# One change to a gated mix of two attentions: the output projection's two halves placed together in every second slot

## The chip, the cores and the metric

The kernel runs on one core of a Trainium2 chip. The metric is the device time of one execution in microseconds (us). Beside plain runs there is one profiled execution, and every row of a trace below comes from it. Engines are named as the profile names them: PE multiplies matrices, PEld loads its weights, DVE, ACT and POOL work on vectors, and SP issues most of the DMAs.

## The reference, cut to what matters

Two attentions read the same `x` (2048 rows, 512 columns, 32 heads of 16) and are mixed row by row with a gate. A works in four blocks of 512 rows with a causal mask and adds a memory term; B is plain attention over all 2048 rows.

```python
g = _sigmoid((x * gate_w).sum(-1, keepdims=True))
a = _A_ref(x, A_wq, A_wk, A_wv, A_wo, A_beta)   # (softmax(q k^T/4 + mask) v, mixed with memory) @ wo
b = _B_ref(x, B_wqkv, B_wo)                     # softmax(q k^T/4) v  @ wo
return g * a + (1 - g) * b
```

The last step of each attention is a projection by a 512x512 matrix (`A_wo`, `B_wo`). The gate is applied to the rows ahead of it, so one row block of the output is the sum of two projections, one for A and one for B. These are the two "halves" of the title.

## The kernel before, in words

After a first part that makes queries, keys and values (up to 335 us in the trace), the work goes through 32 **slots**, `k` = 0 to 31. A slot handles one B unit and one A unit; a unit is four heads of one block of 512 query rows. Within a slot, 37 **groups** follow each other, all issued by the same loop over `n`, so that the order on every engine is the order of this program text:

- groups 0 to 31 are of the B unit, 32 to 36 of the A unit. Each begins with `t_group` (L516 to L538): two matmuls, one for each of two heads, write scores into two PSUM banks (L528), and ACT takes their exponentials into `raw` (L534). On A units POOL then masks (L537).
- Then come tasks from `plan`. In most groups that is one `s_b` (L467 to L476) for the next slot's B unit: a pair of score matmuls into a bank pair `sbk` (L474) and a maximum over them on DVE (L476, rows with `mxb`). In A groups it is `s_a` (L442 to L463).
- Then come the tasks of `ex[k][0]`, made by `extras` (L876). **The output projection is one of them.**
- Then `pv` (L540 to L551) multiplies exponentials with values into one bank, `pvb` (L550). In group 0 this ends the A unit of the slot before, and `fin_copy` (L553) copies the bank out on DVE (L557, `pvs`). In group 1 there is no `pv` in slots 1 to 30; from group 2 on there is one for the new B unit.

The scores and the projection share three PSUM banks, `T3` (two `tb` and one `mb`). `bank` and `misc` hand out the one used longest ago, so a new user waits until the last reader of that bank is done.

The projection has these parts:

- `out_split(c, t)` (L608): at the end of every even slot from 8 on, ACT copies 128 normalised rows for A and B to `oh` (L609, 128x1024) and POOL takes the remainder into `ol` (L610).
- `out_mm(c, t, a)` (L612): twelve matmuls into one bank (L616), `oh` with the weights' high part `wh`, then `oh` with `wl`, then `ol` with `wh`, four each. For `a` = 0 ACT copies the bank to `yo` (L620). For `a` = 1 DVE adds the bank to `yo` (L623) and SP stores 128 output rows (L624).

Before the change, slot `k` from 9 to 30 runs one half in group 1: `a` = 0 in odd slots, `a` = 1 in even ones. Slot 31 runs one half in group 1 and the other in group 28. The last four row blocks have a path of their own behind the slots (`tail_mm`).

Other steps that the prediction names: `fin_load`, `fin_rec`, `fin_bc` and `fin_norm` (L563 to L595) bring a finished unit's sums through DRAM and normalise them (DVE L574 to L578, POOL L590 and L595); `m_chain` (L480) makes the maxima of the next slot in four short DVE operations (L485 to L495).

Of the kernel before, what the change touches and what calls it, by code (L numbers as in the profile page):

```python
# [29 lines left out]
OMI = 14  # L30
# [4 lines left out]
def gated_mix_kernel(ctx, tc, xt, wq, wk, wv, wo, beta, wqkv, wob, gate_w, out):  # L35
# [622 lines left out]
    def todo(fn, *a):  # L658
        return lambda: fn(*a)
# [90 lines left out]
    for blk in range(16):  # L750
# [9 lines left out]
        n = blk + 1 + (c == 2)  # L760
# [114 lines left out]
    def extras(k):  # L875

        pre, post = {}, {}
        if not k:
            for n in range(4):
                pre[2 * n] = [fill[n - 4]]  # L880
        post[2 * S_LAST + 4] = [todo(m_rows, k + 1)]
        for n, at in [(k - 9, 1)] + [(23, 2 * OMI)] * (k == 31):
            if n >= 0:
                pre[at] = [todo(out_mm, n // 8, n // 2 % 4, n % 2)]
        return pre, post

    def beside(k, it):
# [26 lines left out]


    ex = [extras(k) for k in range(32)]
    plan = {}

# [103 lines left out]
```

## Time and profile before

| | us |
|---|---|
| median of 3 runs | 1959.34 |
| lowest, highest | 1958.81, 1960.34 |
| the profiled execution's own time | 1956.4 |
| its span, first to last instruction | 1954.7 |
| begin of slot 0, begin of slot 31 | 335.36, 1883.63 |

The span is cut into slots at the first score matmul of a B unit that follows one of an A unit. A row of a timeline gives the start in us from the span's start, the duration, the engine, the line of the kernel, the operation with what it writes and reads, the shape, the number of merged instructions, and in brackets how long the engine had been idle and whose end it waited for. A row of a table by stretches gives begin and end, the length, and then each engine's busy time with its instruction count.

### The profile page before, as it was taken

The numbers are of one execution on the slowest core, as the hardware profiler recorded it, in microseconds if no ns is written. First come the engines' busy times: TensorE is split into PE (matmuls) and PEld (weight loads), VectorE is DVE, ScalarE is ACT, GpSimd is POOL, SyncE is SP. The second block draws the span as 40 slices with busy tenths as digits, with TensorE's granted clock in tenths as the row PEclk, the third lists the DMA queues.
The fourth block names the chain that finished last, engine by engine and source line by source line (L and its number), as shares of the span: only waits on it lengthen the run. The fifth ranks groups of instructions, "written<-read, shape, count | busy, mean of one in ns | idle before, by whom it ended". The sixth has DMA issues, their size and how long they took to land.

```text
span 1954.7 us, 43539 instructions
## 1 busy us (share of the span) xinstructions
PE 1930.3 (99%) x17485; PEld 939.3 (48%) x17485; DVE 1629.9 (83%) x1798; ACT 1433.4 (73%) x2699; POOL 275.8 (14%) x497
## 2 busy tenths in 40 slices
PE   7999999999999999999999999999999999999999
PEld 5887777444344444444444444444444444444445
DVE  7135766899999999999999999999999999999942
ACT  4233333688888888888888888888888888888884
POOL 5201000012120101111111111111111111111022
PEclk9999999999999999999999999999999999999999
DMA  7666655644444444343435453444354444434111
GB/s 218 170 205 188 198 192 178 156 98 115 98 115 93 106 91 109 81 111 80 114 87 115 87 115 87 113 87 115 87 115 87 109 86 96 101 88 106 48 50 58
DMA packets 163790, 222.49 MB, mean 114 GB/s; under 512 B 39916, under 2 KB 90556, under 8 KB 157828
## 3 DMA queue, kind: packets, MB, share of 16 engines
q1 hardware_dynamic: 159284, 211.41, 43.7%
q0 software_dynamic: 3248, 8.03, 2.1%
q8 instruction: 138, 2.26, 0.5%
q14 instruction: 64, 0.52, 0.1%
q10 hardware_dynamic: 1056, 0.26, 0.1%
HBM read 147.95 MB, written 68.16 MB: 111 GB/s over the span
## 4 chain that ended last, share of the span: by engine, by line
PE 95%; DVE 3%; ACT 1%; SPq 1%; DMA 1%; issue 0%; DVEq 0%; ACTq 0%
PE pvb L550 33%; PE tb L528 17%; PE sbk L474 12%; PE mb L528 9%; PE tb L304 4%; PE sbk L452 3%; PE tb L616 2%; PE mb L304 2%; PE sbk L287 1%; DVE mxb L476 1%; PE tb L287 1%; PE pvb L304 1%; PE mb L616 1%; PE sbk L456 1%; PE mb L287 1%; PE pvb L287 1%
## 5 line engine op out<-in xcount | busy, mean ns | idle before, releaser
L476 DVE TENSOR_REDUCE mxb<-sbk 128x2 f32<-128x1024 f32 x1024 | 1222.3, 1222 | 67.3 <-PE sbk L474 63.1
L534 ACT ACTIVATE raw<-tb 128x512 f32<-128x512 f32 x1555 | 887.5, 598 | 152.9 <-PE tb L528 89.6
L550 PE MATMUL pvb<-raw,vb 128*17 128x256 f32 (+1 forms) x8072 | 639.3, 388 | 0.0
L534 ACT ACTIVATE raw<-mb 128x512 f32<-128x512 f32 x782 | 467.6, 598 | 79.5 <-PE tb L528 44.8
L528 PE MATMUL tb<-qb,xh 64*128 64x512 f32 x872 | 331.6, 495 | 1.7 <-ACT raw L534 1.7
L550 PEld LDWEIGHTS pvb<-raw,vb 128*17 128x17 f32 x8072 | 134.4, 95 | 340.1 <-issue 336.6
L474 PE MATMUL sbk<-xh,qb 64*128 64x512 f32 x1344 | 281.5, 395 | 2.7 <-DVE mxb L476 1.8
L528 PE MATMUL mb<-qb,xh 64*128 64x512 f32 x445 | 220.6, 496 | 0.0
L537 POOL TENSOR_SCALAR_AFFINE_SELECT raw<-raw 128x256 f32<-128x256 f32 (+1 forms) x320 | 115.5, 361 | 709.6 <-ACT raw L534 701.7
L528 PEld LDWEIGHTS tb<-qb,xh 64*128 64x128 f32 x872 | 124.7, 183 | 179.6 <-issue 89.9
L528 PE MATMUL tb<-qb,kb 64*128 64x512 f32 x470 | 179.5, 496 | 1.3 <-DVE st L314 0.8
L460 DVE TENSOR_REDUCE mx<-sbk 128x2 f32<-128x768 f32 (+1 forms) x128 | 136.7, 1090 | 22.9 <-PE sbk L456 18.3
L474 PE MATMUL sbk<-kb,qb 64*128 64x512 f32 x704 | 146.4, 398 | 0.0
L474 PEld LDWEIGHTS sbk<-xh,qb 64*128 64x128 f32 x1344 | 138.3, 186 | 7.4 <-DVE mxb L476 5.0
L528 PEld LDWEIGHTS mb<-qb,xh 64*128 64x128 f32 x445 | 81.3, 183 | 95.2 <-issue 50.4
L590 POOL TENSOR_TENSOR o<-o,d 128x512 f32<-128x512 f32 x31 | 39.7, 1281 | 545.6 <-DMA d<-rd 461.9
L528 PEld LDWEIGHTS tb<-qb,kb 64*128 64x128 f32 x470 | 68.2, 183 | 100.1 <-issue 52.6
L528 PE MATMUL mb<-qb,kb 64*128 64x512 f32 x234 | 116.1, 496 | 0.0
L550 PE MATMUL pvb<-raw,va 128*17 128x256 f32 (+2 forms) x1280 | 94.7, 384 | 0.8 <-ACT pvs L559 0.8
L452 PE MATMUL sbk<-ka,qa 64*128 64x256 f32 (+3 forms) x512 | 88.2, 358 | 1.1
L528 PE MATMUL tb<-qa,ka 64*128 64x512 f32 (+3 forms) x339 | 79.5, 372 | 0.0
L311 ACT ACTIVATE st<-tb 128x512 fp32r<-128x512 f32 x33 | 19.8, 599 | 80.2 <-DVE phi L310 40.5
(284 smaller groups left out, 1837.6 us busy)
## 6 DMA issues: line engine op xcount, KB each, us to landing
xh<-dB SPq DMA_DIRECT2D x38, 512.0 KB
vb<-vdB SPq DMA_DIRECT2D x16, 1088.0 KB
dB<-st SPq DMA_DIRECT2D x64, 256.0 KB
dA<-st SPq DMA_DIRECT2D x64, 256.0 KB
pd<-pvs SPq DMA_DIRECT2D x64, 256.0 KB
kb<-dB SPq DMA_DIRECT2D x22, 512.0 KB
xh<-dB SPq DMA_DIRECT2D x38, 256.0 KB
qb<-dB SPq DMA_DIRECT2D x64, 128.0 KB
```

Source lines behind the costliest of these rows:

```text
L287: nc.tensor.matmul(b, lhs, WV[wi][:, k, :], start=n == 0, stop=n == 11)
L304: nc.tensor.matmul(b, WS[ws][w][wi][:, k, :], (XH, XL)[xi][c][:, k, :], start=n == 0, stop=n == 11)
L452: nc.tensor.matmul(b[:, j, c0:c0 + n], q_of(u)[r, p, i * 128:(i + 1) * 128], k_of(u, p)[r, :n], start=True, stop=False)
L460: nc.vector.tensor_reduce(m[:, :, p, i], b[:, :, :n], axis=AX.X, op=OP.max)
L474: nc.tensor.matmul(b[:, j], q_of(u)[r, p, i * 128:(i + 1) * 128], k_of(u, p)[r, kc * C:(kc + 1) * C], start=True, stop=True)
L476: nc.vector.tensor_reduce(MXB[u][:, :, p, i, kc], b, axis=AX.X, op=OP.max)
L528: nc.tensor.matmul(bs[j][:, c0:c0 + w], k_of(u, h // 2)[r, 128 * it:128 * it + 128], q_of(u)[r, h // 2, q0:], start=True, stop=True)
L534: nc.scalar.activation(pt, bs[j], AF.Exp, scale=SCALE)
L537: nc.gpsimd.affine_select(out=m, in_=m, pattern=[[1, 128]] if n < 2 else [[0, 2], [1, 128]], compare_op=OP.is_ge, fill=0.0, base=0, channe ...
L550: nc.tensor.matmul(PVB[32 * h:32 * h + E + 1, q0 + lo:q0 + hi], vt[:, it, 4 * q + h, :], pt[:, lo:hi], start=it == 0 and lo == 0, stop=it ...
L590: nc.gpsimd.tensor_tensor(o, o, d, op=OP.mult)
L616: nc.tensor.matmul(b, (AT["oh"], AT["ol"])[oi][:, g, a], (AT["wh"], AT["wl"])[wi][:, g, a], start=n == 0, stop=n == 11)
```

## The change: what it does

`extras` no longer puts one half of a projection into group 1 of every slot. It puts both halves, one right behind the other, into group 1 of every odd slot from 9 to 29, and none into the even slots from 10 to 30. In slot 31 the first half stays in group 1 and the second in group 28. No operation is added or removed. Eleven second halves move, each from group 1 of an even slot to group 1 of the odd slot ahead of it.

```diff
-        for n, at in [(k - 9, 1)] + [(23, 2 * OMI)] * (k == 31):
-            if n >= 0:
-                pre[at] = [todo(out_mm, n // 8, n // 2 % 4, n % 2)]
+        n = k - 9
+        if n >= 0 and n % 2 == 0:
+            for a, at in enumerate((1, 1 if k < 31 else 2 * OMI)):
+                pre.setdefault(at, []).append(todo(out_mm, n // 8, n // 2 % 4, a))
```

Since banks are handed out in turn, names of banks rotate by one in the groups between the two places. On PE, this is slot 9 from its group 0 to the scores of its group 2 before the change (`tb_110`, `tb_111` and `mb` are the three shared banks):

```order
L528 MATMUL mb<-qb_70,kb_89 128x512
L528 MATMUL tb_111<-qb_70,kb_89 128x512
L474 MATMUL sbk_114<-xh_87,qb_68 128x512 x2
L550 MATMUL pvb<-raw_86,va_76 17x256 x4
L528 MATMUL tb_110<-qb_70,kb_89 128x512
L528 MATMUL mb<-qb_70,kb_89 128x512
L474 MATMUL sbk_115<-xh_87,qb_68 128x512 x2
L616 MATMUL tb_111<-wh,oh 128x512 x4
L616 MATMUL tb_111<-wl,oh 128x512 x4
L616 MATMUL tb_111<-wh,ol 128x512 x4
L528 MATMUL tb_110<-qb_70,kb_89 128x512
L528 MATMUL mb<-qb_70,kb_89 128x512
```

From the same place on, with the change (from the scores of group 1 to those of group 2):

```order
L528 MATMUL tb_110<-qb_70,kb_89 128x512
L528 MATMUL mb<-qb_70,kb_89 128x512
L474 MATMUL sbk_115<-xh_87,qb_68 128x512 x2
L616 MATMUL tb_111<-wh,oh 128x512 x4
L616 MATMUL tb_111<-wl,oh 128x512 x4
L616 MATMUL tb_111<-wh,ol 128x512 x4
L616 MATMUL tb_110<-wh,oh 128x512 x4
L616 MATMUL tb_110<-wl,oh 128x512 x4
L616 MATMUL tb_110<-wh,ol 128x512 x4
L528 MATMUL mb<-qb_70,kb_89 128x512
L528 MATMUL tb_111<-qb_70,kb_89 128x512
```

The second half's twelve matmuls now stand behind the first half's and write the bank whose exponential belongs to group 1's first score matmul. PE in slot 10, from its group 0 to the scores of its group 2, before:

```order
L528 MATMUL tb_111<-qb_68,xh_87 128x512
L528 MATMUL tb_110<-qb_68,xh_87 128x512
L474 MATMUL sbk_114<-xh_88,qb_69 128x512 x2
L550 MATMUL pvb<-raw_86,va_76 17x256 x4
L528 MATMUL mb<-qb_68,xh_87 128x512
L528 MATMUL tb_111<-qb_68,xh_87 128x512
L474 MATMUL sbk_115<-xh_88,qb_69 128x512 x2
L616 MATMUL tb_110<-wh,oh 128x512 x4
L616 MATMUL tb_110<-wl,oh 128x512 x4
L616 MATMUL tb_110<-wh,ol 128x512 x4
L528 MATMUL mb<-qb_68,xh_87 128x512
L528 MATMUL tb_111<-qb_68,xh_87 128x512
```

and with the change, from group 0 to the end of group 2:

```order
L528 MATMUL tb_110<-qb_68,xh_87 128x512
L528 MATMUL mb<-qb_68,xh_87 128x512
L474 MATMUL sbk_114<-xh_88,qb_69 128x512 x2
L550 MATMUL pvb<-raw_86,va_76 17x256 x4
L528 MATMUL tb_111<-qb_68,xh_87 128x512
L528 MATMUL tb_110<-qb_68,xh_87 128x512
L474 MATMUL sbk_115<-xh_88,qb_69 128x512 x2
L528 MATMUL mb<-qb_68,xh_87 128x512
L528 MATMUL tb_111<-qb_68,xh_87 128x512
L474 MATMUL sbk_114<-xh_88,qb_69 128x512 x2
L550 MATMUL pvb<-raw_86,vb_2773 17x256 x4
```

Group 2's scores now follow group 1's with only the pair of `sbk` matmuls between them. From slot 31 on the two programs have the same order on PE, with the same banks.

## The prediction

> **What bounds the kernel now.** I read the page first: which engine has no room.
>
> ```profile
> PE 1930.3 (99%) x17485; PEld 939.3 (48%) x17485; DVE 1629.9 (83%) x1798; ACT 1433.4 (73%) x2699; POOL 275.8 (14%) x497
> PEclk9999999999999999999999999999999999999999
> PE 95%; DVE 3%; ACT 1%; SPq 1%; DMA 1%; issue 0%; DVEq 0%; ACTq 0%
> ```
>
> PE is busy for 99% of the span at full clock, and 95% of the chain that ended last is PE's. The change adds no PE work, so the question is whether PE waits more or less. A page's average can't tell that. I therefore cut the trace into slots and asked for each engine's busy time in three sets: slots 1 to 8 (no projection), the odd slots 9 to 29 (first halves), and the even slots 10 to 28 (second halves; slot 30 is left out because it has fewer maxima). Columns are begin and end, length, then busy time of PE, PEld, DVE, ACT and POOL.
>
> ```profile
> 446.09:493.79 47.70, 47.38 (x497) 19.26 (x494) 45.66 (x47) 40.67 (x76) 9.90 (x17) 1.00 0.53 120
> 493.79:542.27 48.48, 47.41 (x496) 19.09 (x492) 46.52 (x47) 40.74 (x76) 7.34 (x15) 1.00 0.41 97
> 733.07:781.06 47.99, 47.67 (x496) 19.41 (x493) 45.92 (x47) 40.66 (x77) 6.17 (x13) 1.00 0.45 107
> sum 382.68, PE 379.36 PEld 154.04 DVE 366.40 ACT 325.46 POOL 54.03; mean PE 47.42 PEld 19.25 DVE 45.80 ACT 40.68 POOL 6.75
> ...
> sum 553.12, PE 552.73 PEld 235.94 DVE 507.56 ACT 461.90 POOL 66.04; mean PE 50.25 PEld 21.45 DVE 46.14 ACT 41.99 POOL 6.00
> ...
> sum 500.78, PE 500.44 PEld 212.56 DVE 468.02 ACT 408.83 POOL 74.56; mean PE 50.04 PEld 21.26 DVE 46.80 ACT 40.88 POOL 7.46
> ```
>
> Without slots 3 and 8 (48.48 and 47.99, see the rivals), a slot with no projection takes (382.68 - 48.48 - 47.99) / 6 = 47.70 us. An odd slot takes 553.12 / 11 = 50.28, an even one 500.78 / 10 = 50.08. A first half thus lengthens its slot by 2.58 us and a second half by only 2.38. The reader is to see that the two prices differ and that in empty slots PE has some 0.3 us more idle time (47.70 against 47.38). **The even slots' projection hides a stall.** The next view shows where: PE's timeline at the head of slot 6, which has no projection.
>
> ```profile
> 637.67 0.50 PE L528 MATMUL mb<-qb,kb 64*128 64x512 f32 x1
> 638.89 0.50 PE L528 MATMUL tb<-qb,kb 64*128 64x512 f32 x1
> 639.46 0.39 PE L528 MATMUL tb<-qb,kb 64*128 64x512 f32 x1
> 640.13 0.50 PE L528 MATMUL tb<-qb,kb 64*128 64x512 f32 x1 [0.29 <-ACT raw L534]
> 641.35 0.50 PE L528 MATMUL mb<-qb,kb 64*128 64x512 f32 x1
> ```
>
> Group 0 starts at 637.67, group 1 at 638.89. Group 1 has no `pv`, so group 2 starts only 0.57 later, at 639.46. Its second score matmul then waits until 640.13, because with three banks it needs the one that group 1 wrote first, and ACT has to read that:
>
> ```profile
> 639.48 0.60 ACT L534 ACTIVATE raw<-tb 128x512 f32<-128x512 f32 x1 [0.20 <-PE tb L528]
> ```
>
> That exponential ends at 639.48 + 0.60 = 640.08. From group 0 to group 3 an empty slot takes 641.35 - 637.67 = 3.68 us. Now the same stretch with one half in group 1, in slot 9 (first half) and in slot 10 (second half):
>
> ```profile
> 781.06 0.50 PE L528 MATMUL mb<-qb,kb 64*128 64x512 f32 x1
> ...
> 783.11 1.19 PE L616 MATMUL tb<-wh,oh 128*128 128x512 f32 x4
> 784.14 1.08 PE L616 MATMUL tb<-wl,oh 128*128 128x512 f32 x4
> 785.06 1.08 PE L616 MATMUL tb<-wh,ol 128*128 128x512 f32 x4
> 786.07 0.50 PE L528 MATMUL tb<-qb,kb 64*128 64x512 f32 x1
> ...
> 787.29 0.52 PE L528 MATMUL tb<-qb,kb 64*128 64x512 f32 x2
> ```
>
> ```profile
> 831.32 0.50 PE L528 MATMUL tb<-qb,xh 64*128 64x512 f32 x2
> ...
> 833.20 1.19 PE L616 MATMUL tb<-wh,oh 128*128 128x512 f32 x4
> 834.23 1.07 PE L616 MATMUL tb<-wl,oh 128*128 128x512 f32 x4
> 835.14 1.07 PE L616 MATMUL tb<-wh,ol 128*128 128x512 f32 x4
> 836.14 0.50 PE L528 MATMUL mb<-qb,xh 64*128 64x512 f32 x1
> ...
> 837.35 0.50 PE L528 MATMUL tb<-qb,xh 64*128 64x512 f32 x1
> ```
>
> Slot 9's stretch is 787.29 - 781.06 = 6.23, slot 10's 837.35 - 831.32 = 6.03. A half in slot 10 occupies PE from 833.20 to 836.14, that is 2.94, but lengthens the stretch by only 6.03 - 3.68 = 2.35. The other 0.59 is the stall above, in which PE would have waited for ACT anyway. The rest of a slot is the same with or without a half: 47.70 - 3.68 = 44.02, 50.28 - 6.23 = 44.05, 50.08 - 6.03 = 44.05.
>
> **The change part by part.** *Removed: the second half from eleven even slots (10 to 30).* Each stretch falls from 6.03 back to 3.68, a gain of 2.35 us. It is not 2.94: what is late next is group 2's bank, and the 0.59 stall stands open again.
>
> *Added: a second half right behind the first in eleven odd slots.* Here nothing is left to hide it: the exponentials of group 1 are done while the first half runs. No row of before shows two halves in a row, so I bound the price from two sides. Lower: the pace inside a half in slot 10 is 835.14 - 834.23 = 0.91 for four matmuls, so 12 take 2.73. Upper: in the first part of the kernel, chains of twelve matmuls of the same shape (L287, full 128 rows, 512 columns, each into another bank) follow each other without a wait:
>
> ```profile
> 62.33 2.02 PE L287 MATMUL sbk<-wv,xh 128*128 128x512 f32 x8
> ...
> 65.11 2.02 PE L287 MATMUL sbk<-wv,xh 128*128 128x512 f32 x8
> ...
> 67.88 2.02 PE L287 MATMUL tb<-wv,xh 128*128 128x512 f32 x8
> ```
>
> They start 2.78 and 2.77 apart. I take 2.74, near the row of the same instruction.
>
> *The sum for a pair of slots*: + 2.74 - 2.35 = **+0.39 us**; with the bounds, and 2.38 or 2.35 for the gain, + 0.35 to + 0.43. Eleven pairs: 11 x 0.39 = **+4.3 us** (3.9 to 4.7).
>
> The Trainium skill, TensorE: Matmul & The Clock Gate, section Back-to-back issue gap, gives 216 ns for an isolated matmul of 512 columns and 131 ns for one in a stream. By the first, an estimate, the second half would cost 2.59 and the sum would be + 2.6 us; by the second, 1.57 and - 8.6 us. The rows above, 0.91 for four, say 228 ns, and no run here shows either figure; the measurement decides.
>
> *Waits that the second half brings.* Its bank is the one group 1 wrote first, whose exponential ends before the first half does: in slot 9 ACT is through with both of group 1's at 783.37 + 0.59 = 783.96 (the first row below), 2.1 us before PE goes on from the first half at 786.07. It costs nothing. Behind the halves, group 2 needs the first half's bank; ACT reads it in 0.60 under the 2.74 of the second. Group 3 needs the second half's bank, which DVE adds out of:
>
> ```profile
> 783.37 0.59 ACT L534 ACTIVATE raw<-mb 128x512 f32<-128x512 f32 x1
> 786.18 0.60 ACT L620 ACTIVATE yo<-tb 128x512 f32<-128x512 f32 x1 [2.21 <-PE tb L616]
> ```
>
> ```profile
> 836.31 0.69 DVE L623 TENSOR_TENSOR yo<-tb,yo 128x512 f32<-128x512 f32 x1 [1.26 <-PE tb L616]
> ```
>
> In slot 10 the addition ends at 837.00, 0.35 ahead of group 3 at 837.35; the distance is the same in an odd slot, as nothing else stands in DVE's queue. Queued behind it is group 2's maximum, as in slot 10 now. No cost. If that cover went, at most the 0.69 would show, + 7.6 over eleven pairs.
>
> *DVE and ACT* have 1.6 us (47.70 - 46.11, an even slot's 46.80 less the addition) and 7 us of room in an empty slot, as slots 1 to 8 show with nearly the same work.
>
> *Stores and loads.* SP's store of 128 rows moves from an even slot's head to the odd slot before. It goes in between the store of `pvs` and the loads of a finished unit, and SP stands idle there:
>
> ```profile
> 833.95 0.34 SPq L561 DMA_DIRECT2D pd<-pvs  x1
> 837.03 0.36 SPq L624 DMA_DIRECT2D out_dram<-yo  x1
> 845.01 0.53 SPq L567 DMA_DIRECT2D o<-pd  x1
> ```
>
> In the odd slot it would be issued some 8.7 us after the slot's begin; the loads behind it follow at 12 to 15 us (845.01 - 831.32 = 13.69 here). Nothing waits for it. The loads feed two reciprocals on DVE, which come 2.35 us earlier in an even slot than now; in slots 1 to 8 they come as early and none waited, since the one wait in 63 is at the very end:
>
> ```profile
> L574 DVE RECIPROCAL rec<-rec 128x16 f32<-128x16 f32 x63 | 15.3, 243 | 12.2 <-DMA rec<-pd 12.2
> ```
>
> **The rivals.** *The stall doesn't come back (not slower).* Place: group 2 of the even slots. If ACT were ahead there, the whole 0.59 would vanish, a pair would change by 0.39 - 0.59 = - 0.20, and the sum would be - 2.2 us, 1957.1. From 0.39 missing on, the change is no longer slower; from 0.04 missing on, it is under the 0.2% (3.9 us) that a measurement of this kernel can tell from no change. For it: no empty slot after slot 9 has been seen. Against it: slots 1 to 8 have the same queues on ACT ahead of it, and their lengths agree to 0.1 us where nothing else happens. As a whole unlikely, in part quite possible: 27%.
>
> *The second half is cheaper than the first (within 0.2%).* Under 2.71 us, a pair would cost less than 0.36 and the sum less than 3.9. But the L287 chains show 2.77 for a chain behind a chain, not less than the pace inside one: 3%. The skill's 216 ns would put this case at 1961.9.
>
> *The two halves overlap on PE (faster).* They write different banks. If half of the second, 1.37, lay beside the first, a pair would change by 1.37 - 2.35 = - 0.98 and the sum by - 10.8 us, 1948.5. The chains of L287 write different banks too and don't overlap: 4%. The skill's 131 ns in a stream would be such a case, with 1950.7.
>
> *The short slots lose other cover (slower still).* Slot 3 took 0.78 longer than its like and slot 8 0.29, both without a projection. In slot 3 a short DVE operation of `m_chain` was stretched to 1.28 us while POOL copied weights:
>
> ```profile
> 522.23 1.28 DVE L495 SCALAR_TENSOR_TENSOR m<-mx,mhi 128x32 f32<-128x32 f32 x1
> ```
>
> In even slots POOL's product L590 runs near `m_chain`:
>
> ```profile
> 1258.20 1.28 POOL L590 TENSOR_TENSOR o<-o,d 128x512 f32<-128x512 f32 x1 [24.74 <-DMA d<-rd]
> ```
>
> ```profile
> 1263.31 0.21 DVE L485 TENSOR_REDUCE mx<-mxb 128x16 f32<-128x64 f32 x1
> ```
>
> `m_chain` comes 2.35 us earlier and L590 follows DMAs; 1263.31 - 1259.48 = 3.8 us part them now. If in each even slot they met, 0.78 x 11 = 8.6 would come on top: 1972.2. With slot 8's 0.29 each, + 3.2: 1966.8. L590 waits for DVE's reciprocals, which come earlier as well, so 10%.
>
> That the change doesn't do what it says is excluded: the rows of the order above show both halves together.
>
> **How the numbers follow.** The profiled execution took 1956.4, the runs 1959.34 in the median; I add the sum to both, 1960.7 and **1963.6**. The forecast, a pair slower by 0.35 to 0.43, has 56%: 1963.2 to 1964.0. The stall partly or wholly gone, or a cheaper second half: 30%, 1957.1 to 1963.2. Overlap: 4%. Lost cover: 10%, 1966.8 to 1972.2. The range 1960.5 to 1967.0 leaves out the lower half of the second case (some 10%), the overlap, and the worse part of the lost cover. Slower by over 0.2%: 56 + 10 = 66%; within: 30%; faster: 4%. The forecast lies just past the bound, + 0.22%.
>
> **What would show it.** In the changed kernel's trace, the even slots should be 47.7 us long with 3.68 from group 0 to group 3, and with PE's wait for `raw` in group 2. The odd slots should be near 53.0, with 8.97 in that stretch, 24 matmuls of L616 without a gap in the middle, and the second twelve 2.74 long. Even stretches below 3.3 would prove the first rival; a second half under 2.71 the second, under 2 the overlap; even slots above 48, with a stretched DVE row or a wait for a DMA, the last.

## The result and the profile after

The changed kernel took **1964.24 us** in the median of 14 runs (1960.87 to 1968.66), against 1960.19 for the kernel before (14 runs). The ratio is **1.0022, with a 95% interval of 1.0015 to 1.0030**: slower by about 4 us, as forecast (+4.3). The interval lies clear of 1, but whether the loss is above 0.2% it leaves open.

The page after shows PE as the engine without room, as before, with one point less:

```profile
span 1961.2 us, 43538 instructions
PE 1931.6 (98%) x17485; PEld 944.2 (48%) x17485; DVE 1624.8 (83%) x1798; ACT 1432.7 (73%) x2699; POOL 275.6 (14%) x497
```

Cut by slots, first the odd ones from 9 to 29 (eleven), then the even ones from 10 to 28 (ten), then all of slots 9 to 30:

```profile
sum 583.25, PE 582.86 PEld 261.26 DVE 513.86 ACT 463.19 POOL 66.22; mean PE 52.99 PEld 23.75 DVE 46.71 ACT 42.11 POOL 6.02
...
sum 477.59, PE 474.39 PEld 193.51 DVE 456.88 ACT 407.11 POOL 74.35; mean PE 47.44 PEld 19.35 DVE 45.69 ACT 40.71 POOL 7.43
...
782.91:1889.79 1106.88, 1102.96 (x11069) 473.52 (x11066) 1002.08 (x1033) 910.69 (x1695) 147.94 (x265) 1.00 0.42 95
```

The last row answers to this one of before:

```profile
781.06:1883.63 1102.57, 1101.81 (x11070) 469.20 (x11066) 1008.08 (x1033) 911.16 (x1695) 148.06 (x265) 1.00 0.42 95
```

An odd slot now takes 583.25 / 11 = 53.02 us (50.28 before), an even one 477.59 / 10 = 47.76 (50.08). The 22 slots together grew by 1106.88 - 1102.57 = **4.31 us**, the forecast sum. PE's busy time in them grew by only 1.15; the rest, 3.2 us, is idle time of PE. The waits of PE in these slots say where 3.1 of it lies:

```profile
PE tb L528 <- ACT raw L534: 2.0, 7, 0.3
PE mb L528 <- ACT raw L534: 1.1, 4, 0.3
```

A row gives who waited for whom, the us in total, the times and the longest. These are eleven waits of 0.27 to 0.29, one in each even slot; the same view of before has no row of PE at all. The span grew by 6.5; the other 2.2 lie where the two programs are the same, 0.8 ahead of slot 0, 1.0 in slots 0 to 8 and 0.4 from slot 31 on. So below I compare the 22 slots and not spans.

PE at the head of slot 11, from group 0 to group 3, with both halves:

```profile
883.52 0.49 PE L528 MATMUL tb<-qb,xh 64*128 64x512 f32 x1
...
885.57 1.21 PE L616 MATMUL mb<-wh,oh 128*128 128x512 f32 x4
886.62 1.08 PE L616 MATMUL mb<-wl,oh 128*128 128x512 f32 x4
887.54 1.08 PE L616 MATMUL mb<-wh,ol 128*128 128x512 f32 x4
888.45 1.07 PE L616 MATMUL tb<-wh,oh 128*128 128x512 f32 x4
889.36 1.07 PE L616 MATMUL tb<-wl,oh 128*128 128x512 f32 x4
890.27 1.07 PE L616 MATMUL tb<-wh,ol 128*128 128x512 f32 x4
891.26 0.50 PE L528 MATMUL tb<-qb,xh 64*128 64x512 f32 x1
...
892.49 0.51 PE L528 MATMUL tb<-qb,xh 64*128 64x512 f32 x2
```

The stretch is 892.49 - 883.52 = 8.97 us. Between the halves there is no gap. The first four matmuls take 1.05 to the next four, then fours start 0.91 to 0.92 apart across the border of the halves, and the last four take 0.99 to group 2's scores. And slot 12, which is empty now:

```profile
936.48 0.50 PE L528 MATMUL tb<-qb,kb 64*128 64x512 f32 x2
938.27 0.39 PE L528 MATMUL tb<-qb,kb 64*128 64x512 f32 x1
938.95 0.50 PE L528 MATMUL mb<-qb,kb 64*128 64x512 f32 x1 [0.29 <-ACT raw L534]
940.16 0.50 PE L528 MATMUL tb<-qb,kb 64*128 64x512 f32 x2
```

The stretch is 940.16 - 936.48 = 3.68, and group 2's second score matmul waits for ACT, as in slots 1 to 8 before.

The other steps of the prediction, in slot 11: DVE's addition and SP's store.

```profile
891.43 0.69 DVE L623 TENSOR_TENSOR yo<-tb,yo 128x512 f32<-128x512 f32 x1 [4.17 <-issue]
```

```profile
892.15 0.36 SPq L624 DMA_DIRECT2D out_dram<-yo  x1
895.43 0.53 SPq L567 DMA_DIRECT2D o<-pd  x1
```

The addition ends at 892.12, 0.37 ahead of group 3 at 892.49. The store goes out 8.6 us after the slot's begin, 3.3 ahead of the next load.

### The profile page after: what moved, and what is told of

Read it like the earlier page. It is cut to its first block, busy times and chain, and to the rows that moved or that the text cites. A ratio compares the mean times of both kernels' runs of the same rounds, so it can differ in the third digit from the quotient of the medians.

```text
span 1961.2 us, 43538 instructions
## 1 busy us (share of the span) xinstructions
PE 1931.6 (98%) x17485; PEld 944.2 (48%) x17485; DVE 1624.8 (83%) x1798; ACT 1432.7 (73%) x2699; POOL 275.6 (14%) x497
## 4 chain that ended last, share of the span: by engine, by line
PE 93%; DVE 3%; DMA 2%; ACT 1%; issue 0%; SPq 0%; DVEq 0%; ACTq 0%
PE pvb L550 32%; PE tb L528 17%; PE sbk L474 12%; PE mb L528 9%; PE tb L304 4%; PE sbk L452 3%; PE tb L616 2%; PE mb L304 2%; DVE mxb L476 1%; PE sbk L287 1%; PE pvb L304 1%; PE tb L287 1%; PE mb L616 1%; PE sbk L456 1%; PE pvb L287 1%; PE mb L287 1%
## 5 line engine op out<-in xcount | busy, mean ns | idle before, releaser
L528 PE MATMUL tb<-qa,ka 64*128 64x128 f32 (+3 forms) x339 | 79.6, 373 | 0.0
```

Source lines behind the costliest of these rows:

```text
L528: nc.tensor.matmul(bs[j][:, c0:c0 + w], k_of(u, h // 2)[r, 128 * it:128 * it + 128], q_of(u)[r, h // 2, q0:], start=True, stop=True)
```

## The experiments

Two questions were left. Is the loss in the even slots (a stall that is open again), or in the odd ones (two halves in a row bring a wait)? And does the stall hang on ACT and the three banks? Ratios are to the kernel before on the same chip; "22 slots" is the length of slots 9 to 30 in the profiled execution, and the medians are over the eleven odd and the eleven even slots of these. PE's granted clock in slots 9 to 30 is 1.00 in all twelve.

| run | ratio (95%) | 22 slots | odd, even slot (median) |
|---|---|---|---|
| before | | 1102.57 | 50.26, 50.05 |
| the change | 1.0022 (1.0015 to 1.0030) | 1106.88 | 52.96, 47.72 |
| mid | 1.0062 (1.0047 to 1.0077) | 1114.24 | 50.70, 50.67 |
| apart | 1.0041 (1.0025 to 1.0058) | 1110.22 | 53.22, 47.71 |
| even | 1.0016 (1.0003 to 1.0029) | 1104.85 | 47.72, 52.77 |
| short_exp | 1.0020 (1.0010 to 1.0030) | 1105.67 | 52.97, 47.61 |
| after_sfirst | 1.0014 (1.0001 to 1.0028) | 1105.55 | 52.96, 47.58 |
| before_pool | 1.0004 (0.9993 to 1.0015) | 1103.44 | 50.31, 50.08 |
| before_oh | 1.0011 (1.0001 to 1.0020) | 1106.25 | 50.07, 50.62 |
| before_dve | 0.9989 (0.9979 to 0.9998) | 1102.10 | 50.21, 50.05 |
| before_dve_sfirst | 0.9989 (0.9978 to 1.0000) | 1102.09 | 50.17, 50.07 |
| after_dve_sfirst | 0.9996 (0.9986 to 1.0005) | 1104.20 | 52.87, 47.60 |

### mid: one half per slot, where there is no stall

```diff
-        for n, at in [(k - 9, 1)] + [(23, 2 * OMI)] * (k == 31):
+        for n, at in [(k - 9, 10 if k < 31 else 1)] + [(23, 2 * OMI)] * (k == 31):
```

> The kernel before, with each half in group 10 of its slot in place of group 1 (slots 9 to 30). Bank theory: a slot whose group 1 holds no half has a stall of about 0.6 us in group 2, because the third score matmul waits for ACT's exponential; a half in group 1 hides it, a half elsewhere hides nothing. Then every slot has a head stretch (group 0 to 3) of 3.68 us or a little more in odd slots, each half costs 2.7 to 2.9, a pair of slots takes 100.8 to 101.3 in place of 100.36, and the time is 5 to 9 us above before. Place theory (a half costs the same everywhere): a pair stays at 100.3 to 100.4 and the time is that of before within 2 us.

The time is 0.62% above before, and the 22 slots take 1114.24 - 1102.57 = 11.7 us more, above the 5 to 9 expected (a pair of slots takes 101.4, just above the 101.3 expected). PE in slot 12, the head first, then group 10:

```profile
938.40 0.49 PE L528 MATMUL mb<-qb,kb 64*128 64x512 f32 x1
...
940.86 0.49 PE L528 MATMUL tb<-qb,kb 64*128 64x512 f32 x1 [0.29 <-ACT raw L534]
...
942.08 0.50 PE L528 MATMUL mb<-qb,kb 64*128 64x512 f32 x1
...
950.66 0.49 PE L528 MATMUL tb<-qb,kb 64*128 64x512 f32 x1
...
951.34 1.20 PE L616 MATMUL tb<-wh,oh 128*128 128x512 f32 x4
952.38 1.08 PE L616 MATMUL tb<-wl,oh 128*128 128x512 f32 x4
953.30 1.08 PE L616 MATMUL tb<-wh,ol 128*128 128x512 f32 x4
954.31 0.63 PE L550 MATMUL pvb<-raw,vb 128*17 128x256 f32 x8
954.87 0.50 PE L528 MATMUL tb<-qb,kb 64*128 64x512 f32 x1
```

The head is 3.68 with the stall in it. The half occupies PE for 954.31 - 951.34 = 2.97, and group 10 takes 954.87 - 950.66 = 4.21 in place of 1.24 (947.58 - 946.34 in slot 12 before): all 2.97 show. So the place decides, and the theory that a half costs the same everywhere falls. A lone half costs 2.97 without cover, and 2.38 (second half) or 2.58 (first) in group 1.

### apart: both halves in the odd slot, not in a row

```diff
-            for a, at in enumerate((1, 1 if k < 31 else 2 * OMI)):
+            for a, at in enumerate((1, 10 if k < 31 else 2 * OMI)):
```

> The changed kernel with the second half nine groups later in the same odd slot (group 10 in place of group 1). Bank theory: the second half has no stall to hide in either place, so it costs 2.7 to 2.9 again; odd slots 52.9 to 53.2, even ones 47.7, time within 2 us of the changed kernel, 4 to 6 us above before. Burst theory (the loss is a wait that two halves in a row bring on banks, DVE or ACT): odd slots fall to 52.6 and the time to that of before.

Odd slots grew to 53.22 and even ones stayed at 47.71. The theory that two halves in a row bring a wait falls: pulled apart they cost 0.26 us more in each odd slot, and the 22 slots 3.3 more than with the change (0.6 of it in slot 10 alone, which took 48.34). That is also more than the 2 us I had allowed. A half that begins behind other work pays for going in and out: in mid and here 2.97 and 2.94, against 2.70 (52.96 - 50.26) right behind another half. The rows of mid above show it at both ends: the first four matmuls take 1.04 to the next four and the last four 1.01 to `pv`, in place of some 0.91. The change saves this once per pair, and still loses.

### even: both halves in the even slots

```diff
-        n = k - 9
+        n = k - 9 if k == 31 else k - 10
```

> The changed kernel with both halves in the even slots 10 to 30 in place of the odd ones (slot 31 as it was). The copy to oh on ACT still opens the odd slots, which are empty now. Bank theory: even slots take 47.70 + 2.35 + 2.73 = 52.8; odd slots are longer than an empty 47.70, by 0.2 to 0.5, because the copy delays the exponentials on which the stall hangs; a pair takes 100.7 to 101.0, and the time is 4 to 7 us above before. If the stall doesn't hang on ACT, odd slots take 47.70 and a pair 100.5.

Even slots took 52.77, as worked out. Odd ones took 47.72, so here my expectation missed: the copy to `oh` does not lengthen an empty slot. It is the length that I had put down to a stall that doesn't hang on ACT. The 22 slots are 2.3 us above before, not 4 to 7. ACT in slot 11 shows another reason:

```profile
883.29 1.06 ACT L609 ACTIVATE oh<-o 128x1024 fp32r<-128x1024 f32 x1
884.24 0.60 ACT L534 ACTIVATE raw<-tb 128x512 f32<-128x512 f32 x1
884.71 0.61 ACT L534 ACTIVATE raw<-mb 128x512 f32<-128x512 f32 x1
885.30 1.09 ACT L534 ACTIVATE raw<-tb 128x512 f32<-128x512 f32 x2
```

Group 0's exponentials are late by some 0.2 us, but group 1's begin at 885.30, 1.81 after the slot's begin at 883.49. In the changed kernel's empty slot 12 they begin at the same distance, 938.30 - 936.48 = 1.82, and there ACT had been idle for 0.20:

```profile
938.30 0.60 ACT L534 ACTIVATE raw<-mb 128x512 f32<-128x512 f32 x1 [0.20 <-PE mb L528]
```

The copy's delay fits into that idle time, so these rows agree with a stall that hangs on group 1's exponentials alone; the next run tests that. This layout's 22 slots are 2.0 us shorter than the change's (1104.85 against 1106.88), as a slot with both halves takes 52.77 without the copy at its head and 52.96 with it.

### short_exp: half of one exponential left out

ACT takes only 256 of the 512 columns of group 1's first exponential in the even slots 10 to 30; the other half of the columns isn't computed.

```diff
-            nc.scalar.activation(pt, bs[j], AF.Exp, scale=SCALE)
+            w = 256 if (kd, n, j) == ("B", 1, 0) and u in range(42, 63, 2) else C
+            nc.scalar.activation(pt[:, :w], bs[j][:, :w], AF.Exp, scale=SCALE)
```

> The changed kernel, leaving out half the columns of the first exponential of group 1 in the even slots 10 to 30 (ACT reads 256 of 512 columns). PE's work is the same. Bank theory: that exponential takes some 0.2 us less, and the stall in group 2 shrinks by 0.15 to 0.25 us, so that the head stretch of even slots goes from 3.68 to about 3.47 and the time falls by 2 to 3 us against the changed kernel (1 to 2.5 us above before). If group 2 waits for something else (the maxima on DVE, the pvb bank), the stretch stays at 3.68 and the time at that of the changed kernel.

PE and ACT in slot 12 (the added line moves the numbers by one):

```profile
936.17 0.50 PE L528 MATMUL tb<-qb,kb 64*128 64x512 f32 x2
...
938.43 0.49 PE L528 MATMUL mb<-qb,kb 64*128 64x512 f32 x1
...
939.64 0.50 PE L528 MATMUL tb<-qb,kb 64*128 64x512 f32 x2
```

```profile
937.99 0.38 ACT L535 ACTIVATE raw<-mb 128x256 f32<-128x256 f32 x1 [0.20 <-PE mb L528]
```

The exponential takes 0.38 in place of 0.60. PE's matmul follows its end by 0.06, at 938.43, and the stretch falls to 939.64 - 936.17 = 3.47, as the bank theory said. It is the only edit, and it is on ACT: that the stall hangs on this exponential is shown. The whole slot fell by less, from 47.72 to 47.61, because group 3 gave some back (1.31 in place of 1.22); why it did is not shown. The 22 slots fell by 1.2 us, under the 2 to 3 expected.

### after_sfirst: other work of PE ahead of the stall

```diff
+            early_s = n == 2 and k in SFIRST
+            if early_s:
+                for f in plan.get((k, n), []):
+                    f()
             t_group(*(ub, n) if n < 2 * NT else (ua, n - 2 * NT), banks)
-            for f in plan.get((k, n), []) + ex[k][0].get(n, []):
+            for f in ([] if early_s else plan.get((k, n), [])) + ex[k][0].get(n, []):
                 f()
```

`SFIRST` holds slots 1 to 8 and the even ones from 10 to 30.

> The changed kernel, and in group 2 of each slot without a half in group 1 (1 to 8, and the even ones from 10) the pair of sbk matmuls is issued ahead of the group's scores in place of behind them. No work is added. Bank theory: PE's stall there is a wait for a bank that ACT still reads, so other PE work that needs no such bank fits into it; the head stretch falls from 3.68 by about the pair's 0.33, to 3.3 to 3.45, slots without a half take 47.4, and the time falls by 4 to 6 us against the changed kernel (19 slots by 0.23 to 0.33), so that it is at or just under that of before. If DVE's maxima set the pace there, the pair waits for its sbk bank, nothing falls, and the time stays 4 us above before.

The empty slots fell to 47.58, by 0.14 and not by 0.23 to 0.33, and their head to 3.49, not to 3.3 to 3.45. The 22 slots fell by 1.3 us against the change, and the time stayed above before (1.0001 to 1.0028), where I had expected it to be level. PE and ACT in slot 12:

```profile
939.62 1.00 PE L474 MATMUL sbk<-xh,qb 64*128 64x512 f32 x4
940.46 0.39 PE L528 MATMUL tb<-qb,kb 64*128 64x512 f32 x1
940.53 0.50 PE L528 MATMUL mb<-qb,kb 64*128 64x512 f32 x1
940.95 0.67 PE L550 MATMUL pvb<-raw,vb 128*17 128x256 f32 x8
```

```profile
940.37 1.12 ACT L534 ACTIVATE raw<-tb 128x512 f32<-128x512 f32 x2
```

```profile
940.95 0.17 PEld L550 LDWEIGHTS pvb<-raw,vb 128*17 128x17 f32 x8 [0.25 <-DVE pvs L557]
```

```profile
939.98 0.68 DVE L557 COPY pvs<-pvb 128x512 f32<-128x512 f32 x1
```

The second score matmul no longer waits long, but `pv` follows at 940.95, and it needs both of group 1's exponentials, of which the second starts at 940.37 and takes 0.59 alone, so it ends at 940.96. The profile names DVE's copy of the bank as what ended the wait, but that copy was done at 940.66. By these times a second wait on ACT stands behind the bank; no run tests it by itself. Reordering PE's work recovers a fourth of the stall (0.14 of 0.59); twelve matmuls in front of both waits cover all of it.

### before_pool, before_oh, before_dve: the odd slots' 0.2 us

These three leave one half per slot and move the copy to `oh`, to see why a first half costs 0.2 us more than a second.

```diff
-        nc.scalar.activation(AT["oh"], o_cols(c, t), AF.Copy)
+        nc.gpsimd.tensor_copy(AT["oh"], o_cols(c, t))
```

> The kernel before, with the copy to oh on POOL in place of ACT. The odd slots' 0.2 us over the even ones (50.26 against 50.05) come from the 1.06 us copy that opens them on ACT, if that is right: odd slots fall to 50.05 and the time by 2.3 us. But POOL then does copy and remainder one after the other, some 1.2 and 2.4 us behind its masks, so the remainder may be ready only 4 us after the slot's begin, about when its matmuls start: then the odd slots gain nothing or lose up to 0.3 and the time stays within 3 us of before.

Nothing is gained, by the second of the two ways: in slot 11 the last four matmuls wait for the remainder, which POOL begins after its copy.

```profile
893.54 0.77 PEld L616 LDWEIGHTS mb<-wh,ol 128*128 128x128 f32 x4 [0.35 <-POOL ol L610]
```

In before_oh the copy stays on ACT but is issued behind group 33:

```diff
+        if k >= 8 and k % 2 == 0 and it == NT:
+            out_hi(k // 8 - 1, k // 2 % 4)
```

> The kernel before, with the copy to oh issued on ACT three groups earlier (behind group 33, among the A unit's exponentials), the remainder on POOL where it was. If the odd slots' 0.2 us are the wait for this copy, they fall to 50.05 us and the time by 2.3 us, provided ACT has room among the A groups (it idles 0.4 to 0.6 us twice there). If it has not, the even slots grow by up to 0.5 and the time by up to 3 us.

Odd slots fell to 50.07, the length of an even one before, so the 0.2 us are ACT's copy ahead of the exponentials. Even slots grew by 0.57, as ACT has no room for it among the A groups, and the 22 slots by 3.7 us, where I had allowed 3. In slot 12 a score matmul of the A unit waits for ACT, 47.39 us after the slot's begin where it had stood at 46.80:

```profile
983.17 0.18 PEld L528 LDWEIGHTS tb<-qa,ka 64*128 64x128 f32 x1 [0.33 <-ACT raw L534]
```

The third way is DVE (`nc.vector.tensor_copy`), which was profiled twice:

> The kernel before, with the copy to oh on DVE in place of ACT. DVE idles 0.96 us at a slot's begin and 2 us beside a half. If the odd slots' 0.2 us are ACT's copy ahead of the exponentials, odd slots fall from 50.26 to 50.05 and the time by 2.3 us (0.12%), as nothing here makes POOL's remainder late. If the copy in DVE's queue holds up the first maximum by more than DVE's idle time covers, odd slots stay at 50.2 or grow.

> The same kernel as the run beside it, a second look: its profile shows whether the odd slots' length repeats within 0.05 us.

Odd slots fell only to 50.21 (50.18 in the second profiled execution). The median of the runs fell by 0.11%, about as expected, but the 22 slots by 0.5 us only and not by 2.3, so most of that fall is not the remedy's. In slot 11, POOL's last masks explain a part; the first fence is the kernel before, the second before_dve:

```profile
881.00 0.90 POOL L537 TENSOR_SCALAR_AFFINE_SELECT raw<-raw 128x256 f32<-128x256 f32 x2 [0.61 <-ACT raw L534]
```

```profile
889.03 1.21 POOL L537 TENSOR_SCALAR_AFFINE_SELECT raw<-raw 128x256 f32<-128x256 f32 x2 [0.61 <-ACT raw L534]
```

Beside DVE's copy two masks take 1.21 us in place of 0.90, and group 0's `pv` needs them; the slot's first group takes 890.85 - 889.55 = 1.30 in place of 1.22.

### The two remedies together

> The kernel before (one half per slot) with both remedies: the copy to oh on DVE, and the sbk pair ahead of group 2's scores in slots 1 to 8. By the parts: eleven odd slots by 0.21 and eight slots by 0.13, together 3.3 us under before, ratio 0.9983. If the two don't add, about 2.3.

> The changed kernel with the same two remedies, the second in slots 1 to 8 and in the even ones from 10: odd slots 52.96 - 0.2, nineteen slots 47.58, together 4.7 us under the changed kernel, so about 0.5 us under before and 2.8 above the run with one half per slot.

With one half per slot the time is 0.11% below before, at the edge of its interval; in the profile, slots 0 to 8 gained 1.0 us (444.69 against 445.70) and the 22 slots 0.5, together 1.5, under the 2.3 to 3.3 expected. With both halves in odd slots the time is that of before, about as expected, and the 22 slots stay 2.1 us longer than with one half per slot (1104.20 against 1102.09). So the remedies do not turn the order of the two layouts around. A version clearly faster than both was not found.

## Why the prediction was right

- *The bound.* PE sets a slot's length, and what it waits more lies at one place: eleven waits for ACT's exponential, 3.1 us, which before had not. Its busy time rose by 1.15 us in 22 slots, the length by 4.31.
- *The removed half* was to give back 2.35, not 2.94. Measured: 50.08 - 47.76 = 2.32 per slot, and the stretch is the 3.68 of an empty slot. short_exp shows that the wait there is ACT's exponential.
- *The added half* was priced at 2.74 from its own pace and the chains of L287. Measured: 53.02 - 50.28 = 2.74 per slot; from group 0 to group 3 alone, 2.71 to 2.76 in ten of the eleven slots and 3.02 in slot 17. The figures of 216 and 131 ns that the prediction cites did not come up: 888.45 to 889.36 is 228 ns for each of four.
- *The sum* of + 0.39 a pair and + 4.3 us was met: 4.31 in the trace, ratio 1.0022. That it was met to 0.01 us is luck. The stretches from group 0 to group 3 alone grew by 4.46 in the 22 slots, and the rest of these slots fell by 0.15, as single slots of either program run some 0.3 longer than their like.
- *No new waits* in the odd slots, on banks, DVE or SP: the addition's distance to group 3 is 0.37 against the 0.35 worked out, and PEld's waits for it add up to 4.7 us in both programs (3.4 and 1.3, eleven in all).
- *The rivals.* The stall did come back, in all eleven even slots. The second half cost 2.74 by the means of the slots and 2.70 by their medians: that is near the second rival's edge of 2.71, but the sum did not fall under its 3.9. The halves don't overlap. Even slots lost no other cover: eight of the ten from 10 to 28 took 47.65 to 47.73, and two (20 and 28) some 0.27 more. In each of these one score matmul starts 0.27 to 0.28 later, behind an exponential of ACT, as one did in slot 15 before; what delays it was not tried.

The working did not name one thing, though the sum holds it: the change also saves. A lone half pays 0.24 to 0.27 us for going in and out, which two in a row pay once. Were it not for this, the loss would have been near that of apart, 7.7 us. Why a chain's entry and exit cost this was not tried.

A rule of the Trainium skill, Perfetto Trace Analysis, section Optimization Strategy, fits the cause: the same gap again and again on the engine that should be full can mean too little SBUF or PSUM for the next tile. Here it is a wait of PE for one of three shared banks, in every empty slot: 0.29 us of idle time in its row, and 0.59 in price by the prediction's stretches. No run had a fourth bank, so that part is not tried.

## What to carry to other kernels

Work that looks movable may stand in a stall of the very engine it runs on. Price it at its place, as the length of a stretch with it less that of the same stretch without it, and not at its own duration. Joining two pieces saves an entry (some 0.25 us here) and opens a stall again (some 0.6 here): which is larger is read from stretches of one trace.

## What the runs showed of the hardware

- **The clock in the first part differs between executions.** The begin of slot 0 lay between 335.2 and 343.3 us, with the same program text ahead of it. The granted clock over that part is the third column from the right; before_dve, then a second execution of the same kernel:

```profile
0.00:343.31 343.31, 326.14 (x1553) 255.61 (x1554) 178.32 (x282) 110.92 (x229) 55.46 (x94) 0.98 0.65 189
```

```profile
0.00:335.17 335.17, 320.45 (x1554) 251.42 (x1554) 178.75 (x282) 110.83 (x229) 55.59 (x94) 1.00 0.65 193
```

  That is 8 us, twice the effect of this change, between two executions of one kernel, and a reason to compare stretches of slots. Shorter stretches show that the low mean is half clock for a few us, here in before_dve and then in the second execution:

```profile
45.56:52.39 6.83, 6.83 (x45) 6.10 (x44) 1.29 (x2) 2.23 (x4) 2.42 (x5) 1.00 0.96 163
52.39:59.22 6.83, 6.83 (x21) 5.57 (x21) 0.43 (x2) 0.18 (x1) 3.23 (x7) 0.50 0.82 188
```

```profile
52.39:59.22 6.83, 6.83 (x33) 5.66 (x34) 0.46 (x2) 0.18 (x1) 4.18 (x8) 1.00 0.86 209
```

  In the same stretch PE gets through 21 matmuls at half clock and through 33 at full clock. The traces without half clock ahead of slot 0 (one), with 3.4 us of it (four) and with 13.7 us (four) begin slot 0 at 335.2, at 335.4 to 336.2 and at 341.7 to 343.3 us, and the other four lie between. A clock gate that watches PE's activity, as in the Trainium skill, TensorE: Matmul & The Clock Gate, section The HAM clock gate, could do this: it says that the clock falls to half after an idle window of some 3.4 us. No idle window of that kind stands in the rows: in the 6.83 us ahead of the half clock the profile counts PE as busy throughout. What does stand there are 32 matmuls of a single column each (L203, from 49.49 us on). They stand in the second execution too, without half clock behind them, so what sets it off stays open.
- **A copy on DVE slows masks on POOL**: two masks take 1.21 us in place of 0.90 beside a copy of 0.70. Whether the copy is slowed too is not shown, as no run has it alone. The Trainium skill, Perfetto Trace Analysis, section Optimizing Scalar/DVE Operations, says that the two engines share a read port to SBUF; these rows agree.
